# Block-wise linear attention and a gated MLP on one core: two tokens to a row, 64x64 attention tiles, and one written order for every engine

## The chip, the core and the metric

The kernel runs on one core of a Trainium2 chip. The metric is the time of one execution on the device, in microseconds (us), the median of several. The core's engines run side by side and wait for each other by semaphores: TensorE (PE: matmuls, results into PSUM; PEld is its loading of weights), VectorE (DVE), ScalarE (ACT), GpSimd (POOL, which is given no operand in PSUM here), and SyncE (SP), which issues transfers. PSUM has eight banks of 512 fp32 columns on 128 partitions.

## What is computed

Inputs are q, k, v of shape (4 batches, 8 heads, 768 tokens, 64) in fp32, a decay `lam` for each head, and the weights of a gated MLP. The attention has no softmax; a state of 64x64 per head carries the past. In blocks of 64 tokens:

```python
intra = einsum('bhic,bhjc->bhij', qb, kb) * Dmask      # lam ** (i-j) where i >= j, else 0
intra = einsum('bhij,bhjd->bhid', intra, vb)
inter = einsum('bhid,bhde->bhie', qb * lam_pow, kv_state)
out[block] = intra + inter
kv_state = lam ** 64 * kv_state + einsum('bhsd,bhse->bhde', kb * rev_pow, vb)
```

Both kernels take 128 tokens as a block, which gives the same sums. The heads are joined to x of (4, 768, 512), and then:

```python
h = maximum(x @ w_in, 0)                    # 512 -> 1024
u, v = h[..., :512], h[..., 512:]
v_n = (v - mean) / sqrt(var + 1e-6)         # over the 512 features
v_s = einsum('ts,bsd->btd', w_spatial, v_n) + b_spatial[None, :, None]
out = (u * v_s) @ w_out                     # 512 -> 512
```

The mix over tokens (`v_s`) needs all 768 tokens of a batch, so it can start only when the attention of the batch's last tokens is done.

## The kernel before

The work is cut into 12 steps of 256 tokens, three to a batch (`NR`), each of two chunks of 128 tokens (`c`). A step goes through these functions:

- `load_step` (L65): SyncE issues the transfers of q, k and v, fp32, 1.5 MB a step. For k and v a partition holds one token of each chunk, so the runs are 64 floats, 256 bytes (L72, L77). For q a partition holds two neighbouring tokens, 512 bytes (L74). Four steps' inputs fit (`fin`, bufs=4).
- `cast_step` (L144): k times its decay to the block's end becomes `kd` (L150: on VectorE for the first three steps, then on GpSimd); q is cast on ScalarE (L153), v on GpSimd (L154).
- `trans_step` (L157): 16 transposes of 128x128 on PE (L163) into `pt`, a tile of two banks; ScalarE copies the k half (L168), VectorE multiplies the q half by its decay (L170).
- `scores_step` (L177): 16 matmuls with 64 rows, two heads in the two row halves of the array (L189); VectorE applies mask and decay (L192).
- `kv_step` (L198): the chunk's k v sums, 16 matmuls with 64 columns (L207). The state lies in SBUF; VectorE multiplies it by lam^128 (L218) and adds the new sum (L219).
- `out_step` (L222): state times q (L242) on the two diagonal 64x64 tiles, and masked scores times v (L249), added in PSUM; ScalarE writes x transposed (L252).

Then the MLP: `pv` (L269) and `pu` (L292) multiply by the halves of w_in, with the statistics of v on VectorE (L282 to L288). `wt_piece` (L329) transposes w_spatial once. `pvs` (L301) mixes over tokens, for each of 4 groups of 128 features in two halves of 384 tokens: six matmuls and a seventh that adds the bias by a matmul of a constant with the broadcast bias (L309); VectorE multiplies by u (L311). `po` (L316) is the last product; ScalarE evacuates it (L325) and SyncE stores it (L326).

The order on PE and GpSimd is that of the program (`manual_schedule`, L358). In each of its 12 rounds the loop casts step n+2, makes the scores of n+1, the output of n, the state of n+1, and the transposes of n+2; between them `fill` takes MLP pieces from a list, so that the MLP of one batch lies among the attention of the next. The other engines are ordered by the framework's scheduler. The weights are loaded by GpSimd (L108, L360 to L364), cast to bf16 on the way. All PSUM tiles have two banks, four of them in rotation (L54).

Of the kernel before, what the change touches and what calls it, by code (L numbers as in the profile page):

```python
# [13 lines left out]
PE = mybir.EngineType.PE  # L15
# [3 lines left out]
def kernel(  # L19
# [18 lines left out]
    NBLK = S // P  # L38
    NG = H // 2
    NCH = DM // P  # L40
    NR = S // (2 * P)
    NS = B * NR
    T2 = 2 * P
    HW_ = S // 2

    const = ctx.enter_context(tc.tile_pool(name="const", bufs=1))
    wpool = ctx.enter_context(tc.tile_pool(name="wpool", bufs=1))
    fin = ctx.enter_context(tc.tile_pool(name="fin", bufs=4))
    att = ctx.enter_context(tc.tile_pool(name="att", bufs=3))
    gml = ctx.enter_context(tc.tile_pool(name="gml", bufs=1))  # L50
    xpool = ctx.enter_context(tc.tile_pool(name="xpool", bufs=2))
    small = ctx.enter_context(tc.tile_pool(name="small", bufs=2))
    ostg = ctx.enter_context(tc.tile_pool(name="ostg", bufs=3))
    psum = ctx.enter_context(tc.tile_pool(name="psum", bufs=4, space=bass.MemoryType.PSUM))  # L54

    def two_banks(shape, name, dt=FP32):
        return psum.tile(shape, dt, tag="ps", name=name)


    lam_bc = const.tile([P, H], FP32)  # L60
    nc.scalar.dma_start(out=lam_bc, in_=lam.unsqueeze(0).to_broadcast((P, H)))

    st = {}

    def load_step(n):  # L65
        b, r = divmod(n, NR)
        toks = slice(r * T2, (r + 1) * T2)
        q_in = fin.tile([P, H, 2, D], FP32, tag="q_in", name=f"q_in_{n}")
        k_in = fin.tile([P, H, 2, D], FP32, tag="k_in", name=f"k_in_{n}")
        v_in = fin.tile([P, H, 2, D], FP32, tag="v_in", name=f"v_in_{n}")  # L70
        for c in range(2):
            nc.sync.dma_start(out=k_in[:, :, c, :],  # L72
                              in_=k[b, :, toks][:, c * P:(c + 1) * P].rearrange("h p d -> p h d"))
        nc.sync.dma_start(out=q_in.rearrange("p h m d -> p h (m d)"),  # L74
                          in_=q[b, :, toks].rearrange("h (p m) d -> p h (m d)", m=2))
        for c in range(2):
            nc.sync.dma_start(out=v_in[:, :, c, :],  # L77
                              in_=v[b, :, toks][:, c * P:(c + 1) * P].rearrange("h p d -> p h d"))
        st[n] = {"q_in": q_in, "k_in": k_in, "v_in": v_in}

    load_step(0)
    ident = const.tile([P, P], BF16)
    make_identity(nc, ident)

    def iota_f(shape, pattern, base, mult, name):
        ti = const.tile(shape, I32, name=name + "_i")
        nc.gpsimd.iota(ti, pattern=pattern, base=base, channel_multiplier=mult)
        tf = const.tile(shape, FP32, name=name)
        nc.vector.tensor_copy(out=tf, in_=ti)
        return tf  # L90

    krev = iota_f([P, 1], [[0, 1]], P - 1, -1, "krev")

    qpos = iota_f([P, 2, 2, D], [[1, 2], [0, 2], [2, D]], 1, 0, "qpos")

    rel = iota_f([P, 2, D], [[1, 2], [2, D]], 0, -1, "rel")

    win_sb = wpool.tile([P, NCH, DFF], BF16)
    wout_sb = wpool.tile([P, NCH, DM], BF16)
    bsp_bc = wpool.tile([P, S], BF16)  # L100
    wt_sb = wpool.tile([P, NBLK, S], BF16)
    wsp_raw = wpool.tile([P, NBLK, S], BF16)

    def load_win(f0, f1):
        nc.gpsimd.dma_start(out=win_sb[:, :, f0:f1],
                            in_=moe_w_in.rearrange("(g p) f -> p g f", p=P)[:, :, f0:f1])

    load_win(DH, DFF)  # L108
    for n in range(1, 4):
        load_step(n)  # L110


    loglam = const.tile([P, H], FP32)
    nc.scalar.activation(out=loglam, in_=lam_bc, func=AF.Ln)
    logl = const.tile([P, NG], FP32)
    for hh in range(2):
        rows = slice(hh * D, (hh + 1) * D)
        nc.vector.tensor_copy(out=logl[rows, :], in_=loglam[rows, hh::2])
    ldec = const.tile([P, H], FP32)
    nc.scalar.activation(out=ldec, in_=loglam, func=AF.Exp, scale=krev[:, 0:1])  # L120
    lq = const.tile([P, NG, T2], BF16)
    for g in range(NG):
        nc.scalar.activation(out=lq[:, g, :], in_=qpos.rearrange("p m a d -> p (m a d)"),
                             func=AF.Exp, scale=logl[:, g:g + 1])
    l128 = const.tile([P, NG], FP32)
    nc.scalar.activation(out=l128, in_=logl, func=AF.Exp, scale=float(P))
    lm128 = const.tile([P, H], FP32)
    nc.scalar.activation(out=lm128, in_=loglam, func=AF.Exp, scale=-float(P))
    causal = const.tile([P, P], FP32)
    nc.vector.tensor_scalar(out=causal, in0=rel.rearrange("p m d -> p (m d)"), scalar1=0.0,  # L130
                            scalar2=None, op0=ALU.is_ge)
    amask = const.tile([P, 2, 2, 2, P], FP32)
    for h in range(H):
        nc.vector.tensor_scalar(out=amask[:, h // 4, h % 2, (h // 2) % 2, :], in0=causal,
                                scalar1=lm128[:, h:h + 1], scalar2=None, op0=ALU.mult)
    eps_t = const.tile([P, 1], FP32)
    nc.vector.memset(eps_t, 1e-6)
    oo128 = const.tile([P, P], BF16)
    nc.vector.memset(oo128, 1.0 / P)


    xT = {}

    def cast_step(n):  # L144
        s = st[n]
        kd = att.tile([P, 2, H, D], BF16, tag="kd", name=f"kd_{n}")
        qc = att.tile([P, 2, H, D], BF16, tag="qc", name=f"qc_{n}")
        vc = att.tile([P, H, 2, D], BF16, tag="vc", name=f"vc_{n}")
        eng = nc.vector if n < NR else nc.gpsimd
        eng.tensor_tensor(out=kd.rearrange("p c h d -> p h c d"), in0=s["k_in"],  # L150
                          in1=ldec.unsqueeze(2).unsqueeze(3).broadcast_to((P, H, 2, D)),
                          op=ALU.mult)
        nc.scalar.activation(out=qc.rearrange("p m h d -> p h m d"), in_=s["q_in"], func=AF.Copy)  # L153
        nc.gpsimd.tensor_copy(out=vc, in_=s["v_in"])  # L154
        s["kd"], s["qc"], s["vc"] = kd, qc, vc

    def trans_step(n):  # L157
        kd, qc = st[n]["kd"], st[n]["qc"]
        pt = two_banks([P, 2, NG, T2], f"pt_{n}", BF16)
        for j, src in ((0, kd), (1, qc)):  # L160
            for g in range(NG):
                for c in range(2):
                    nc.tensor.transpose(  # L163
                        out=pt[:, j, g, c * P:(c + 1) * P],
                        in_=src[:, c, 2 * g:2 * g + 2, :].rearrange("p h d -> p (h d)"),
                        identity=ident)
# [7 lines left out]
    def qblk(n, g, hh, c):  # L174
        return st[n]["qT"][hh * D:(hh + 1) * D, g, :, c, :]

    def scores_step(n):  # L177


        kT = st[n]["kT"]  # L180
# [237 lines left out]
```

## Time and profile before

| | before |
|---|---|
| time, median of 3 (us) | 184.42 (184.38 to 186.93) |
| span of the profiled execution (us) | 186.7 |
| mean granted clock of TensorE | 0.963 |
| busy us: PE, PEld, DVE, ACT, POOL | 145.7, 96.5, 103.4, 89.1, 34.8 |
| read from and written to memory (MB) | 24.78, 6.29 |
| TensorE matmuls | 1540 |

The page's slices cut the span into 40 equal parts; a digit is the busy share of an engine in a part, in tenths. A line of a timeline has the start in us, the time from first start to last end of the merged instructions, engine, line, operation, output<-inputs, shapes, and in brackets how long the engine stood idle before and what released it. The chain of waits is followed back from the last instruction: at each step to what released it. A matmul's own duration there holds its way through the array; what a matmul costs in a dense row is the distance from start to start.

### The profile page before, as it was taken

The page shows a single profiled execution, that of the slowest core. Times are in us where ns is not written, and L with a number is a line of the kernel's source. Part 1 is how long each engine was busy: PE and PEld are TensorE (multiplying, and loading weights), DVE is VectorE, ACT ScalarE, POOL GpSimd, SP SyncE. Part 2 cuts the span into 40 slices and gives each one's busy share as a digit, 9 for nine tenths or more (in the row PEclk, how much of TensorE's full clock was granted, in tenths as well). Part 3 has the DMA queues.
Part 4 walks back from the last instruction along what each step waited for, and adds up shares of the span by engine and source line. Part 5 has one row for each costly group of instructions (what it writes and reads, how often), then busy time and mean ns, then how long its engine had stood idle before and what let it go on. Part 6 is the DMA issues. An engine that isn't in the chain of part 4 may idle for free.

```text
span 186.7 us, 3638 instructions
## 1 busy us (share of the span) xinstructions
PE 145.7 (78%) x1540; PEld 96.5 (52%) x1540; DVE 103.4 (55%) x191; ACT 89.1 (48%) x98; POOL 34.8 (19%) x35
## 2 busy tenths in 40 slices
PE   0005677507979779999997999999799999999980
PEld 0005563305649556655776665575676646565430
DVE  1029993705399853542989747169884722564400
ACT  4244324712677942268775613666722157660051
POOL 4004060006245344060606005020000000000000
PEclk9999996975999979999999999999999999999999
DMA  4999969999999999999998900530000027000035
GB/s 98 218 211 252 205 161 184 199 212 232 199 241 248 200 239 238 221 225 222 330 254 195 252 8 0 208 133 4 0 0 4 2 79 262 0 0 4 0 132 205
DMA packets 68337, 28.36 MB, mean 152 GB/s; under 512 B 50528, under 2 KB 65248, under 8 KB 68320
## 3 DMA queue, kind: packets, MB, share of 16 engines
q1 hardware_dynamic: 65664, 25.17, 56.5%
q0 software_dynamic: 2512, 2.95, 9.6%
q8 instruction: 12, 0.20, 0.5%
q14 instruction: 5, 0.04, 0.1%
q10 hardware_dynamic: 144, 0.00, 0.0%
HBM read 24.78 MB, written 6.29 MB: 166 GB/s over the span
## 4 chain that ended last, share of the span: by engine, by line
PE 54%; SPq 13%; DVE 11%; ACT 9%; DMA 9%; issue 2%; POOL 1%; ACTq 0%; POOLq 0%
PE pvs L307 17%; PE po L322 11%; DMA v_in<-in_v_dram 9%; PE pv L277 8%; PE pu L297 7%; SPq L77 6%; SPq L72 5%; PE pt L163 4%; DVE a L192 3%; PE pvs L309 3%; SPq L74 3%; DVE st L282 3%; ACT vh L280 2%; ACT wt_sb L336 2%; DVE vn L288 2%
## 5 line engine op out<-in xcount | busy, mean ns | idle before, releaser
L307 PE MATMUL pvs<-wt_sb,vn 128*128 128x384 bf16 x192 | 37.8, 331 | 2.1 <-ACT wt_sb L336 2.0
L192 DVE TENSOR_TENSOR a<-pam,amask 128x1024 bf16<-128x1024 f32 x24 | 28.5, 1210 | 6.0 <-PE pam L189 6.0
L154 POOL CAST vc<-v_in 128x1024 bf16<-128x1024 f32 x12 | 12.9, 1074 | 84.0 <-DMA v_in<-in_v_dram 42.7
L252 ACT ACTIVATE xT<-pat 128x1024 bf16<-128x1024 f32 x12 | 15.8, 1320 | 23.7 <-PE pat L249 23.6
L307 PEld LDWEIGHTS <-vn 128*128 128x128 bf16 x192 | 18.9, 99 | 14.9 <-issue 2.5
L297 PE MATMUL pu<-xT,win_sb 128*128 128x256 bf16 x192 | 24.4, 285 | 1.9 <-DVE a L192 1.9
L311 DVE TENSOR_TENSOR gT<-pvs,uT 128x768 bf16<-128x768 f32 x16 | 15.3, 958 | 18.2 <-PE pvs L309 18.1
L277 PE MATMUL pv<-win_sb,xT 128*128 128x512 bf16 x96 | 24.2, 400 | 1.2 <-ACT xT L252 1.2
L322 PE MATMUL po<-wout_sb,gT 128*128 128x512 bf16 x96 | 21.9, 379 | 1.5 <-DVE a L192 1.1
L297 PEld LDWEIGHTS <-win_sb 128*128 128x128 bf16 x192 | 19.2, 102 | 5.7 <-issue 1.8
L153 ACT ACTIVATE qc<-q_in 128x1024 bf16<-128x1024 f32 x12 | 12.7, 1055 | 19.0 <-DMA q_in<-in_q_dram 19.0
L325 ACT ACTIVATE o<-po 128x1024 f32<-128x1024 f32 x12 | 12.3, 1025 | 19.0 <-PE po L322 19.0
L282 DVE BATCH_NORM_STATS2 st<-vh 128x6 f32<-128x512 bf16 x24 | 15.6, 682 | 10.4 <-ACT vh L280 10.3
L163 PE MATMUL pt<-ident,kd 128*128 128x128 bf16 x96 | 8.6, 242 | 15.5 <-DVE kd L150 15.5
L170 DVE TENSOR_TENSOR qT<-pt,lq 128x1024 bf16<-128x1024 bf16 x12 | 8.2, 684 | 18.5 <-ACT kT L168 18.5
L150 POOL TENSOR_TENSOR kd<-k_in,ldec 128x1024 bf16<-128x1024 f32 x9 | 17.1, 1897 | 6.1 <-DMA k_in<-in_k_dram 6.1
L168 ACT ACTIVATE kT<-pt 128x1024 bf16<-128x1024 bf16 x12 | 12.2, 1021 | 11.2 <-PE pt L163 11.2
L280 ACT ACTIVATE vh<-pv 128x1024 bf16<-128x1024 f32 x12 | 12.3, 1024 | 8.8 <-PE pv L277 8.8
L163 PEld LDWEIGHTS <-kd 128*128 128x128 bf16 x96 | 7.2, 110 | 17.4 <-DVE kd L150 15.7
L277 PEld LDWEIGHTS <-xT 128*128 128x128 bf16 x96 | 9.5, 102 | 11.7 <-issue 1.7
L322 PEld LDWEIGHTS <-gT 128*128 128x128 bf16 x96 | 9.2, 98 | 11.9 <-issue 1.0
L299 ACT ACTIVATE uT<-pu 128x1024 bf16<-128x1024 f32 x12 | 12.2, 1020 | 5.9 <-PE pu L297 5.8
(52 smaller groups left out, 146.2 us busy)
## 6 DMA issues: line engine op xcount, KB each, us to landing
k_in<-in_k_dram SPq DMA_DIRECT2D x24, 256.0 KB, 5.8
q_in<-in_q_dram SPq DMA_DIRECT2D x12, 512.0 KB, 6.1
v_in<-in_v_dram SPq DMA_DIRECT2D x24, 256.0 KB, 6.0
out_dram<-o SPq DMA_DIRECT2D x12, 512.0 KB, 3.4
wsp_raw<-in_moe_w_spatial_dram POOLq DMA_DIRECT2D x1, 1152.0 KB, 11.3
win_sb<-in_moe_w_in_dram POOLq DMA_DIRECT2D x2, 512.0 KB, 8.4
wout_sb<-in_moe_w_out_dram POOLq DMA_DIRECT2D x1, 512.0 KB, 14.8
bsp_bc<-in_moe_b_spatial_dram POOLq DMA_DIRECT2D x1, 192.0 KB, 11.7
```

What stands on the lines that cost most here:

```text
L150: eng.tensor_tensor(out=kd.rearrange("p c h d -> p h c d"), in0=s["k_in"], in1=ldec.unsqueeze(2).unsqueeze(3).broadcast_to((P, H, 2, D)), ...
L154: nc.gpsimd.tensor_copy(out=vc, in_=s["v_in"])
L163: nc.tensor.transpose(out=pt[:, j, g, c * P:(c + 1) * P], in_=src[:, c, 2 * g:2 * g + 2, :].rearrange("p h d -> p (h d)"), identity=ident)
L192: nc.vector.tensor_tensor(out=a_sb[:, i].rearrange("p h g c x -> p (h g) c x"), in0=pam.rearrange("p h g c x -> p (h g) c x"), in1=amask[: ...
L252: nc.scalar.activation(out=xT[b][:, r].rearrange("p g (c d m) -> p (g c) m d", c=2, m=2), in_=po.rearrange("p g c (m d) -> p (g c) m d", m ...
L277: nc.tensor.matmul(out=ps[:, j], lhsT=x[:, r, c, j * P:(j + 1) * P], rhs=win_sb[:, c, DH:DFF], start=(c == 0), stop=(c == NCH - 1))
L280: nc.scalar.activation(out=vh[:, pair, :], in_=ps, func=AF.Relu)
L282: nc.vector.bn_stats(out=m["st6"][:, t, :], in_=vh[:, t, :])
L297: nc.tensor.matmul(out=ps[:, f], lhsT=win_sb[:, c, f * P:(f + 1) * P], rhs=x[:, r, c, :], start=(c == 0), stop=(c == NCH - 1))
L307: nc.tensor.matmul(out=ps[:, i, 0:HW_], lhsT=m["vn"][:, s, f * P:(f + 1) * P], rhs=wt_sb[:, s, cols], start=(s == 0), stop=False)
L311: nc.vector.tensor_tensor(out=m["gT"][:, f, :].rearrange("p (i x) -> p i x", i=2), in0=ps[:, :, 0:HW_], in1=m["uT"][:, f, :].rearrange("p ...
L322: nc.tensor.matmul(out=ps[:, j], lhsT=gT[:, c, t * P:(t + 1) * P], rhs=wout_sb[:, c, :], start=(c == 0), stop=(c == NCH - 1))
```

## The change

The kernel is written anew around four ideas.

*Rows of two tokens.* k, q and v are all loaded with two neighbouring tokens to a partition, in runs of 512 bytes, one load of 512 KB each. A chunk of 128 tokens now lies on 64 partitions, two tokens each; its sums over tokens are done as two matmuls with 64 rows. The columns of w_spatial are transposed with a step of two to fit.

*64x64 attention tiles.* All attention matmuls (`s_c`, `a_v`, `k_v`) use a 64x64 quarter of the array; two heads `o` and two chunks `c` make the four quarters, written to different banks where their rows differ.

*Decays as powers of the position.* v is multiplied at its cast by lam^(384-t) (`v_d`), q at its transpose's evacuation by lam^(t-384) (`e_q`), t counted from the batch's start. Their product has the right power for scores and for the state, so the state needs no decay any more: it is summed in one PSUM bank over the whole batch (`k_v`, bank 7) and only copied out (`s_s`). The mask is 0 and 1.

*One order, written out.* `ORDER` is a list of about 630 operations, each with its step, its bank and its engine; every engine works in this order. PSUM is one tile of eight banks, and each operation names its bank. Evacuations are by single banks and lie on ScalarE or VectorE by the list. `GT` makes GpSimd read an element of a given load before it issues the next weights, so that these come after it.

Besides, the mix over tokens has no bias matmul: VectorE adds the bias in fp32 while it evacuates (`g_b`), and the product with u is an operation of its own, mostly on GpSimd (`g_m`). Inputs are held three deep in place of four.

```diff
+ORDER = """
+LK.0.2.S lam.A pos.P LQ.0.2.S LV.0.2.S LV.1.2.S idn.P LB.6.T msk.P LN.6.A LK.1.2.S KC.0.2.A LL.D LX.A TK.0.6.T
+LQ.1.2.S QC.0.2.P EK.0.6.D LT.0.A TQ.0.6.T LK.2.2.S VD.0.2.P LT.1.A EQ.0.6.D SC.0.1.0.T LT.2.A LQ.2.2.S
...
+SS.0.0.A TQ.1.5.T EK.1.6.A KV.0.1.T LQ.3.2.S GT.0.2.P WI.0.P EQ.1.5.D AV.0.1.0.T SS.0.1.A EX.0.1.1.A
+SC.1.0.2.T KC.2.2.P SC.1.1.4.T EX.0.0.0.A MK.1.0.2.D LV.3.2.S QC.2.2.A GT.1.2.P WI.1.P TK.2.6.T MK.1.1.4.D
...
+"""
...
+    NIN, NCA, NTR, NA, NX, NO, NVS = 3, 2, 2, 2, 3, 4, 2
...
-    psum = ctx.enter_context(tc.tile_pool(name="psum", bufs=4, space=bass.MemoryType.PSUM))
+    ps = psum.tile([P, 8, 512], FP32, name="ps")
+    SB = 7
...
-            nc.sync.dma_start(out=k_in[:, :, c, :],
-                              in_=k[b, :, toks][:, c * P:(c + 1) * P].rearrange("h p d -> p h d"))
+        eng.dma_start(out=dst[n % NIN][:, h0:h1].rearrange("p h m d -> p h (m d)"),
+                      in_=src[b, h0:h1, t].rearrange("h (p m) d -> p h (m d)", m=2))
...
+    def after(e, x, n):
+        nc.gpsimd.tensor_copy(out=seen, in_=(k_in, q_in, v_in)[x][n % NIN][0:1, 0, 0, 0:1])
...
+    def v_d(e, n, x):
+        h = slice(*hx(x))
+        vec(e).tensor_tensor(out=vd[n % NCA][:, h], in0=v_in[n % NIN][:, h],
+                             in1=lv[:, n % NR, h].unsqueeze(3).broadcast_to((P, h.stop - h.start, 2, D)), op=ALU.mult)
...
+    def s_c(e, n, i, b):
+        pa = bank(b, 2).rearrange("p o (w j x) -> p o w j x", w=2, j=2)
...
+                for o in range(2):
+                    for c in range(2):
+                        nc.tensor.matmul(out=pa[row(c), o, w, j], lhsT=kT[n % NTR][row(o), u, j, c * Q64:(c + 1) * Q64],
+                                         rhs=qv(n, o, u, c), start=True, stop=True)
...
+    def k_v(e, n, c):
+        pkv = bank(SB)[:, 0:4 * D].rearrange("p (u d) -> p u d", u=4)
+        new = n % NR == 0 and c == 0
...
+                    nc.tensor.matmul(out=pkv[row(o), u], lhsT=kc[n % NCA][row(c), m, u, o, :],
+                                     rhs=vd[n % NCA][row(c), 4 * o + u, m, :],
+                                     start=new and u == 0 and m == 0, stop=(u == 3 and m == 1),
+                                     skip_group_check=True)
+
+    def s_s(e, n, c):
+        copy(e, s_sb[(2 * n + c) % 4].rearrange("p u d -> p (u d)"), bank(SB)[:, 0:4 * D])
...
-                nc.vector.tensor_tensor(out=sd, in0=prev, in1=lb, op=ALU.mult)
-                nc.vector.tensor_tensor(out=s_sb[:, c], in0=sd, in1=pkv[:, c], op=ALU.add)
...
-            nc.tensor.matmul(out=ps[:, i, 0:HW_], lhsT=oo128, rhs=bsp_bc[:, cols],
-                             start=False, stop=True)
...
+    def g_b(e, bb, f, i, b):
+        HW = S // 2
+        nc.vector.tensor_tensor(out=vsb[(bb * 4 + f) % NVS][:, i * HW:(i + 1) * HW], in0=bank(b)[:, 0:HW],
+                                in1=bsp[:, i * HW:(i + 1) * HW], op=ALU.add)
+
+    def g_m(e, bb, f, i):
...
+        vec(e).tensor_tensor(out=gT[bb % 2][:, f, cols].rearrange("p (a y m) -> p a y m", m=2, y=Q64),
+                             in0=vsb[(bb * 4 + f) % NVS][:, cols].rearrange("p (a y m) -> p a y m", m=2, y=Q64),
+                             in1=uT[bb % 2][:, f, cols].rearrange("p (a m y) -> p a y m", m=2, y=Q64), op=ALU.mult)
...
+    with tc.manual_schedule():
+        for token in ORDER.split():
+            name, *args, e = token.split(".")
+            ops[name](e, *map(int, args))
```

A word of the order is operation, step (or batch), further numbers, bank and engine (A ScalarE, D VectorE, P GpSimd, T TensorE, S SyncE): L loads; KC and QC casts of k and q, VD of v; TK and TQ transposes, EK and EQ their evacuations; SC scores, MK mask; KV states, SS their copy; AV output of the attention, EX its evacuation; PV, PU, PW, PO the products of the MLP, EV, EU, EO their evacuations, BN, RA, RD, VN the normalization, GB bias, GM gate product; WT and EW the transposes of w_spatial; WI, WS, WO, BS the loads of weights and bias; ST stores.

## The prediction

> **What bounds the kernel now.** I read the page's table of engines and its slices first, to see when each engine works.
>
> ```profile
> PE 145.7 (78%) x1540; PEld 96.5 (52%) x1540; DVE 103.4 (55%) x191; ACT 89.1 (48%) x98; POOL 34.8 (19%) x35
> ...
> PE   0005677507979779999997999999799999999980
> ...
> DMA  4999969999999999999998900530000027000035
> ```
>
> TensorE (PE) is nearly full from about the tenth slice (4.67 us each) on and idle or half idle before that, while the DMA engines are full from the second slice to about the 23rd. So there are two stretches with different limits. Next I cut the span into the time before 43.5 us and four pieces after it, of about one batch each (busy time of PE, PEld, DVE, ACT, POOL, then clock, DMA share, GB/s):
>
> ```profile
> 43.50:78.50 35.00, 31.14 (x355) 22.53 (x356) 23.39 (x37) 20.10 (x20) 13.63 (x9) 0.90 1.13 230
> 78.50:113.30 34.80, 33.49 (x385) 22.15 (x380) 23.56 (x44) 20.33 (x22) 8.69 (x6) 1.00 0.85 207
> 113.30:148.00 34.70, 33.40 (x384) 22.25 (x378) 22.54 (x45) 16.63 (x18) 3.93 (x3) 1.00 0.13 47
> 148.00:184.00 36.00, 32.56 (x236) 18.57 (x232) 13.34 (x28) 15.68 (x17) 0.00 (x0) 1.00 0.21 79
> ```
>
> A batch takes 34.8 us and PE is busy 33.4 of it, at full clock: there PE sets the pace, and VectorE with 23 is far behind. Before 43.5 us PE was busy only 145.7 - 130.6 = 15 us, partly at a lower clock. The chain of waits and PE's timeline say why:
>
> ```profile
> 25.91 15.96 DMA v_in<-in_v_dram
> 42.00 1.05 POOL vc L154
> ```
>
> ```profile
> 43.09 0.43 PE L207 MATMUL pkv<-vc,kd 128*64 128x64 bf16 x8 [8.07 <-POOL vc L154]
> ```
>
> The v of step 2 takes 16 us to land, where the median is 6.0. In the records of single packets, 26 to 42 us is the time in which w_spatial, its bias and w_out come in: packets of 256 bytes (18 ns each on one engine) alternate with packets of 1536 or 1024 bytes (134 and 96 ns), so v gets a small part of the engines.
>
> **What the Trainium skill says.** "TensorEngine Tiling (Array Packing)", section Key Properties: tiles of the array load weights and multiply in parallel, and changing the tiling mode drains the engine. The trace agrees on both for two tiles. PE's timeline around one step:
>
> ```profile
> 122.47 0.62 PE L189 MATMUL pam<-qT,kT 64*128 64x128 bf16 x16
> 123.02 0.63 PE L242 MATMUL pat<-qT,s 64*64 64x128 bf16 x16
> 123.59 0.64 PE L249 MATMUL pat<-a,vc 128*64 128x128 bf16 x16
> 124.06 0.42 PE L207 MATMUL pkv<-vc,kd 128*64 128x64 bf16 x16
> 124.41 1.92 PE L297 MATMUL pu<-xT,win_sb 128*128 128x256 bf16 x16
> ```
>
> From start to start the groups of 16 take 0.55, 0.57, 0.47 and 0.35 us. In the trace's single starts two matmuls begin 3.5 ns apart and the next two 56 ns later (32 ns for pkv, 64 columns), whether they are two row halves (L189) or two column halves (L249); where the mode changes, 147 ns pass in place of 56, so a change costs about 0.1 us. Four tiles at once appear nowhere in this trace.
>
> "SBUF — State Buffer", section Who interferes with whom: a VectorE instruction in a two-port mode, or with two SBUF inputs, locks out GpSimd and the reverse; one with at most one SBUF input does not. The trace agrees; GpSimd's timeline, then VectorE's:
>
> ```profile
> 43.81 1.90 POOL L150 TENSOR_TENSOR kd<-k_in,ldec 128x1024 bf16<-128x1024 f32 x1 [0.77 <-DMA k_in<-in_k_dram]
> ...
> 51.16 1.90 POOL L150 TENSOR_TENSOR kd<-k_in,ldec 128x1024 bf16<-128x1024 f32 x1 [0.71 <-DMA k_in<-in_k_dram]
> ```
>
> ```profile
> 44.09 2.09 DVE L288 TENSOR_SCALAR vn<-vh,mv,rstd 128x512 bf16<-128x512 bf16 x2
> ...
> 51.36 1.27 DVE L282 BATCH_NORM_STATS2 st<-vh 128x6 f32<-128x512 bf16 x2
> ```
>
> vn beside kd takes 2.09 us for two in place of 0.73; the statistics beside kd take their usual time.
>
> **The change part by part: PE.** From the same timeline, start to start: pv and po 0.2166 us a matmul, pu 0.1156, pvs 0.1625, transposes 0.0557. Unchanged: 192 x 0.2166 + 192 x 0.1156 + 192 x 0.0557 = 41.6 + 22.2 + 10.7 = 74.5 us. Mixing: 224 matmuls become 192 because the bias moves to VectorE, 36.4 to 31.2 us. Scores: 96 pairs of 64x128 tiles become 96 quads of 64x64 tiles, 5.4 us before and, if four tiles run in the time of two, 5.4 after. Attention times v: the same, 5.4 and 5.4. State times q: 160 matmuls used two diagonal tiles (80 pairs, 4.5 us) and can now use all four (40 quads, 2.2). States: each chunk of 128 tokens is summed as two of 64 rows, so 160 matmuls (80 pairs of 32 ns, 2.5 us) become 320 (5.1). Transposed w_spatial: 2.0 both times. Mode changes: 4 a step, 48, before; 55 in the written order after; 4.8 and 5.5. Sum before 135.5 us, after 131.3. The upper bound for a quad is two pairs after each other, 112 ns: 232 quads x 0.056 = 13 us more. I take 56 ns, because row halves and column halves are each shown to run together.
>
> **The other engines.** Counting the instructions of the order by engine. VectorE: 24 masks x 1.21 (L192), 12 q products x 0.68 (L170), 24 statistics x 0.77 (L282, L283), 24 vn x 0.53 (L288), 32 bias additions of 384 columns (half of L311's 768 in 0.96: 0.56), 12 reciprocals, and 27 evacuations of a bank (0.39 for 256 columns at L215; 0.55 to 0.68 estimated for the wider ones) with four gate products of 0.5: 29.0 + 8.2 + 18.5 + 12.7 + 17.9 + 1.9 + 18.2 = 106 us. What goes is the decay of the state (L218 and L219, 15.8 us) and the gate product at L311. ScalarE: evacuations of 512 columns at about 0.6 (estimated from 1.02 for 1024 and 1.46 for 1536, L168 and L336), in all 80 us. GpSimd: 12 v products x 1.9 (L150), 15 casts x 1.08 (L154), 28 gate products of 384 columns at 0.71 (1.9 x 384/1024), since they read uT with a stride perhaps up to 1.4: 59 to 79 us. None comes near PE's 131. GpSimd at 45% busy holds up only vn and four gate products on VectorE: some 0.2 us each, 6 us. The smaller evacuations lie beside PE as the larger ones do now. The decay tables and masks are made at the start, under the first loads.
>
> **Transfers.** k and v move in runs of 512 bytes in place of 256: 27 ns a packet in place of two of 18. 12 x 3 loads x 1024 packets x 27/16 ns = 62 us of all engines where it was 76. Weights are held back: GpSimd reads one element of a chosen load before it issues them. That is an added wait. Queued behind the first (k of step 2) stand the k cast of step 2, which needs the same load, then v's product of step 2, and PE's transposes wait for the former: it costs nothing while the load it names lands before what is queued behind it could start. The other added hop is in the gate: matmuls, bias on VectorE, product on GpSimd, then po; 0.56 + 0.71 + hops, some 1.4 us against 0.96 now. Behind pvs stand four more halves of the same batch (0.98 each), so it is hidden but for the last one, some 0.5 us.
>
> **The start.** First packet at 2.4 us (now too). A load of 512 KB takes 1.7 us, and k of step 2 is seventh: 14 us. Its cast (1.1), eight transposes (0.45 to 0.9), q's, the product (0.7) and the scores put PE at about 19; half of w_in, released by that load, needs 0.95 for issue and 3.1 alone (512 packets x 96/16), some 4 beside q and v: also 19 to 20. So the first pv runs at 20 us; it is at 29.76 now. From there I let PE run on, with 3.5 us lost: some 2.5 at q of step 3, which shares the engines with weights until about 30 us, and 1 at the lower clock. The whole of w_spatial should be there at 36 us, when PE has just used up the work that does without it.
>
> **The sum.** By 20 us PE has done the attention of steps 0 and 1 and part of 2: 2 x 2.8 + 1.3 = 6.9 us of its 131.3. Left 124.4. 20 + 124.4 + 3.5 + 4.5 (waits in the rest: 4%, as in the windows above) + 4.3 (tail: now 5.2 from the last po to the end, less 0.4 for a half as wide evacuation and 0.5 for a half as large store) = 156.7 us of span. The profiled run is 186.7 where the median is 184.4, so 155 us of time.
>
> **The rivals.**
> *Evacuations hold PE back (167).* VectorE has 25 us of work per batch of some 33, in finer pieces and an order fixed for every engine, so a late one holds what is queued behind it. For it: three waits a batch on the mask product even now (0.93 the longest, before pu at 135.07). Against: ScalarE and GpSimd have room. With 5 us a batch in place of 1.2: +12, 167.
> *Quads run as pairs (168).* +13 us, above. For it: no quad in the trace. Against: the separate pairs.
> *Slower: VectorE and GpSimd shut each other out throughout, or readers of PSUM, now one tile of eight banks, wait for all that was written before.* The first: 106 + 79 + 14 us until data flow = 199. The second: evacuations and PE take turns, 131 + some 138 of evacuation + hops, 270 or more. For the second: the q product waits for the k copy now (18.5 us in all), though they lie in different banks of one tile. Against the first: the lines at 51 us.
>
> **How the numbers follow.** The sum above 0.63, evacuations 0.17, quads as pairs 0.11, slower 0.09. The range from 148 (no waits in the start or later, a weight half 2 us sooner) to 172 (either middle rival with a longer start) leaves out the slow rival and both middle ones together. Faster 0.90, within 2% 0.02, slower 0.08.
>
> **What would show it.** First pv near 20 us; PE's windows of a batch about 33 us; four score matmuls starting within some 15 ns and the next 56 ns later; no load over about 8 us beside the held weights; vn a little over 0.5 us. Wrong would be: waits of PE on the mask, bias or gate products of over 2 us a batch, quads 112 ns apart, or PE idle between 24 and 40 us for want of w_spatial.

## The result and the profile after

The changed kernel takes 161.34 us (median of 4, 159.30 to 162.21) where the kernel before, run beside it, took 185.12: a ratio of 0.866, 95% interval 0.857 to 0.875. Forecast were 155.0 and a range of 148 to 172. Its executions come in two groups, 159.3 us at a mean granted clock of 0.989 and 161 to 162 at 0.979, so ratios compare only the quicker executions of each kernel, and a difference of under 2 us between two versions of it isn't read from a few runs.

The page of the kernel after, engines and slices (4.0 us each):

```profile
PE 138.3 (86%) x2073; PEld 91.0 (57%) x2090; DVE 108.2 (68%) x191; ACT 82.4 (52%) x154; POOL 77.7 (49%) x91
...
PE   1256764999899998999999999999999999999990
...
PEclk9999995699999999999999999999999999999999
...
DMA  3999999999999998266999951530000000134055
```

TensorE is full from the eighth slice on and stays so to the end; before, the fullness began later and was broken in the middle. Slices 6 and 7 are 6 and 4 tenths busy, and the clock of slices 7 and 8 reads 5 and 6. VectorE at 108 us, ScalarE at 82 and GpSimd at 78 are all far from PE. The same cut as before, the start and then about a batch each (busy time of PE, PEld, DVE, ACT, POOL, then clock, DMA share, GB/s):

```profile
0.00:25.90 25.90, 11.57 (x299) 9.76 (x300) 12.03 (x19) 15.95 (x31) 15.07 (x26) 0.97 1.05 248
25.90:62.00 36.10, 34.49 (x513) 23.00 (x519) 28.73 (x50) 21.60 (x38) 16.17 (x18) 0.93 1.11 266
62.00:94.00 32.00, 30.59 (x458) 20.02 (x454) 24.66 (x43) 16.68 (x32) 20.17 (x24) 1.00 0.81 229
94.00:126.00 32.00, 31.68 (x618) 21.47 (x624) 26.19 (x45) 16.08 (x32) 13.76 (x15) 1.00 0.18 65
126.00:155.70 29.70, 29.48 (x205) 16.73 (x208) 16.54 (x35) 11.21 (x21) 12.56 (x12) 1.00 0.21 80
```

After 94 us PE misses 0.5 us in 61.7. The two spans differ by 186.7 - 159.9 = 26.8 us, in three parts: PE runs on from 25.9 us where before it did from 43.5 (17.6); from there to the last `po` it is 130.2 us where it was 138.0 (7.8); the end after that is 3.8 us where it was 5.2 (1.4). Two thirds of the difference thus lie before PE runs on, but not all of that is idle time saved, since PE had been busy 15.1 us by 43.5 in the kernel before and 11.6 by 25.9 in this one. Counted by PE's idle time, the start gives 14.1 us (28.4 to 14.3), about half; 7.4 us are less busy time of PE (145.7 to 138.3), and the rest is fewer waits later and the shorter end.

What ends the start now, from the chain of waits (start, length, what), and PE's timeline there:

```profile
8.84 7.37 DMA k_in<-in_k_dram
16.38 9.47 DMA win_sb<-in_moe_w_in_dram
```

```profile
25.90 0.58 PE L385 MATMUL ps<-win_sb,xT 128*128 128x512 bf16 x1 [3.29 <-DMA win_sb<-in_moe_w_in_dram]
26.70 5.38 PE L385 MATMUL ps<-win_sb,xT 128*128 128x512 bf16 x14 [0.22 <-issue]
```

The v of step 2 is no longer what PE waits for; it is the first half of w_in, for 3.3 us, and behind the wait 16 matmuls of 512 columns take 6.1 us in place of 3.5 (0.2166 each).

The attention's small tiles in the middle of a dense stretch:

```profile
104.84 0.31 PE L350 MATMUL ps<-qT,s_sb 64*64 64x128 bf16 x8
104.98 0.39 PE L359 MATMUL ps<-a_sb,vd 64*64 64x128 bf16 x16
105.20 0.62 PE L313 MATMUL ps<-qT,kT 64*64 64x128 bf16 x32
105.65 0.41 PE L329 MATMUL ps<-vd,kc 64*64 64x64 bf16 x16
```

From start to start, 8 matmuls take 0.14 us, 16 take 0.22, 32 take 0.45. In the single starts four matmuls begin within 10 ns (105.204, .208, .211, .214) and the next four 56 ns later (105.260): four quarters run in the time of two halves.

Three groups off PE (busy us, mean ns of one | idle before it, and what ended it):

```profile
L456 POOL TENSOR_TENSOR gT<-vsb,uT 128x384 bf16<-128x384 f32 x28 | 30.1, 1096 | 28.5 <-DVE vsb L450 23.6
...
L450 DVE TENSOR_TENSOR vsb<-ps,bsp 128x384 f32<-128x384 f32 x32 | 17.3, 549 | 5.6 <-PE ps L445 5.1
...
L414 DVE TENSOR_SCALAR vn<-vh,mv,rstd 128x512 bf16<-128x512 bf16 x24 | 16.5, 723 | 0.3
```

The bias addition costs VectorE 0.55 us, the gate product costs GpSimd 1.10, and vn takes 0.72, since ten of the 24 take 0.68 us or more and the others 0.4.

### The profile page after: what moved, and what is told of

Same layout as the page of the kernel before. It is cut to its first block, busy times and chain, and to the rows that moved or that the text cites. A ratio compares the mean times of both kernels' runs of the same rounds, so it can differ in the third digit from the quotient of the medians.

```text
span 159.9 us, 4876 instructions
## 1 busy us (share of the span) xinstructions
PE 138.3 (86%) x2073; PEld 91.0 (57%) x2090; DVE 108.2 (68%) x191; ACT 82.4 (52%) x154; POOL 77.7 (49%) x91
## 4 chain that ended last, share of the span: by engine, by line
PE 54%; DMA 15%; DVE 12%; SPq 5%; POOL 5%; issue 4%; ACT 3%; DVEq 0%; ACTq 0%; POOLq 0%
PE ps L462 13%; PE ps L423 11%; PE ps L385 10%; PE ps L445 8%; DMA win_sb<-in_moe_w_in_dram 6%; SPq L184 5%; DMA q_in<-in_q_dram 5%; DMA k_in<-in_k_dram 5%; POOL gT L456 4%; DVE vsb L450 4%; PE ps L284 3%; DVE vn L414 3%; PE ps L313 2%; PE ps L329 2%; PE ps L359 2%
## 5 line engine op out<-in xcount | busy, mean ns | idle before, releaser
L456 POOL TENSOR_TENSOR gT<-vsb,uT 128x384 bf16<-128x384 f32 x28 | 30.1, 1096 | 28.5 <-DVE vsb L450 23.6
L445 PE MATMUL ps<-wt_sb,vn 128*128 128x384 bf16 x192 | 33.7, 326 | 0.2 <-DVE vsb L450 0.2
L317 DVE TENSOR_TENSOR a_sb<-ps,m 128x1024 bf16<-128x1024 f32 x24 | 28.7, 1218 | 6.0 <-PE ps L313 5.0
L276 POOL TENSOR_TENSOR vd<-v_in,lv 128x1024 bf16<-128x1024 f32 x12 | 22.8, 1904 | 16.0 <-DMA q_in<-in_q_dram 6.4
L385 PE MATMUL ps<-win_sb,xT 128*128 128x512 bf16 x85 | 24.9, 412 | 4.1 <-DMA win_sb<-in_moe_w_in_dram 3.3
L423 PE MATMUL ps<-xT,win_sb 128*128 128x256 bf16 x192 | 24.2, 273 | 0.3 <-DVE wt_sb L170 0.3
L462 PE MATMUL ps<-wout_sb,gT 128*128 128x512 bf16 x90 | 21.6, 379 | 0.3
L450 DVE TENSOR_TENSOR vsb<-ps,bsp 128x384 f32<-128x384 f32 x32 | 17.3, 549 | 5.6 <-PE ps L445 5.1
L390 ACT ACTIVATE uT<-ps 128x512 bf16<-128x512 f32 x22 | 12.9, 600 | 10.1 <-PE ps L423 10.1
L414 DVE TENSOR_SCALAR vn<-vh,mv,rstd 128x512 bf16<-128x512 bf16 x24 | 16.5, 723 | 0.3
```

The costliest lines, as they stand in the source:

```text
L276: vec(e).tensor_tensor(out=vd[n % NCA][:, h], in0=v_in[n % NIN][:, h], in1=lv[:, n % NR, h].unsqueeze(3).broadcast_to((P, h.stop - h.start ...
L317: nc.vector.tensor_tensor(out=a_sb[n % NA][:, i].rearrange("p o w j x -> p (o w) (j x)"), in0=bank(b, 2).rearrange("p o (w y) -> p (o w) y ...
L385: nc.tensor.matmul(out=bank(b), lhsT=x[:, c, g], rhs=win_sb[:, g, DH:DFF], start=(g == 0), stop=(g == NCH - 1))
L390: nc.scalar.activation(out=o, in_=i, func=AF.Relu)
L414: vec(e).tensor_scalar(out=vn[p2][:, t], in0=vh[p2][:, t], scalar1=mv[p2][:, t, 0:1], scalar2=rstd[p2][:, t:t + 1], op0=ALU.subtract, op1= ...
L423: nc.tensor.matmul(out=pu[:, f2].rearrange("p (c x) -> p c x", c=2), lhsT=win_sb[:, g, f * P:(f + 1) * P], rhs=x[:, :, g, :], start=(g == ...
```

## The experiments

The working theory after the result: the gain is the sum of a shorter start (shorter transfers, held weights) and less PE work (bias, quads). The rival: the written order of the evacuating engines is what carries it, and the parts don't add. (To evacuate is to copy a result from its PSUM bank to SBUF, after which PE may write that bank again; ScalarE and VectorE do it.) All ratios are to the kernel before, run on the same chip. Results per run are medians.

**Quads undone?** The attention loops run over the column halves of one row half first, so that program order holds pairs.

```diff
-            for j in range(2):
-                for o in range(2):
+            for o in range(2):     # in s_c; in a_v the loops become o, i, w and c, i, j, w
+                for j in range(2):
```

> The changed kernel with the same attention matmuls in another order: two column halves of one row half follow each other, so that the next two matmuls use the same two quarters again and only two run at once. Theory (a quad of 64x64 tiles costs what a pair costs, 56 ns, and PE sets the pace): 232 groups of four become 464 of two, 232 x 0.056 = 13 us more, some 174 us. Rival (four tiles gain nothing over two, or PE does not set the pace): no change, within 2 us of 161.

160.87 us, 0.864 (0.855 to 0.873): the same. The timeline says why:

```profile
99.76 0.31 PE L350 MATMUL ps<-qT,s_sb 64*64 64x128 bf16 x8
99.90 0.42 PE L359 MATMUL ps<-a_sb,vd 64*64 64x128 bf16 x16
100.16 0.41 PE L329 MATMUL ps<-vd,kc 64*64 64x64 bf16 x16
```

8 still take 0.14 us and 16 about 0.26: PE starts matmuls of the other row half ahead of their turn. The edit took nothing away, so it doesn't price the quads; the starts above do.

**Bias back on PE**, as a seventh matmul of a constant with the bias in bf16; `g_b` then only copies.

```diff
...
+        nc.tensor.matmul(out=bank(b)[:, 0:HW], lhsT=oo128, rhs=bsp[:, i * HW:(i + 1) * HW],
+                         start=False, stop=True)
...
-        nc.vector.tensor_tensor(out=vsb[...], in0=bank(b)[:, 0:HW], in1=bsp[...], op=ALU.add)
+        nc.vector.tensor_copy(out=vsb[...], in_=bank(b)[:, 0:HW])
```

> The changed kernel with the bias back on PE: a seventh matmul of 384 columns in each of the 32 groups of the mix over tokens, and VectorE only copies. Theory (PE sets the pace from the first pv on): 32 x 0.1625 = 5.2 us more, 166.5 us. Rival (VectorE or GpSimd sets the pace in the mix stage): no change, since VectorE's instruction stays as long as it was.

164.82 us, 0.886 (0.879 to 0.894): 3.5 us slower than the change between the medians, where 32 matmuls of 0.1625 us cost 5.2. The bias's load leaves SyncE's queue by this edit, and the transposes of w_spatial start 1.2 us earlier (42.79 in place of 44.04), which may give part back; no run shows that apart. The term of the sum is shown in kind, its size only roughly.

**Runs of 256 bytes.** Each load as two transfers, one for each token of the row.

```diff
-        eng.dma_start(out=dst[n % NIN][:, h0:h1].rearrange("p h m d -> p h (m d)"),
-                      in_=src[b, h0:h1, t].rearrange("h (p m) d -> p h (m d)", m=2))
+        for m in range(2):
+            eng.dma_start(out=dst[n % NIN][:, h0:h1, m],
+                          in_=src[b, h0:h1, t].rearrange("h (p m) d -> p h m d", m=2)[:, :, m])
```

> The changed kernel with each load of 512 KB issued as two of 256 KB, one per token of a row, so that the runs are 256 bytes. Theory (the start is bound by transfers, 18 against 27 to 32 ns a packet, so a load takes 2.3 in place of 1.8 us): k of step 2, the seventh load, lands some 3.5 us later, the weights that wait for it too, and the first pv runs at about 30 in place of 26 us; 4 to 8 us more, 165 to 169. Rival (the start is bound by the chain of casts, transposes and evacuations): first pv within 1 us of 26 and no change.

178.27 us, 0.957 (0.946 to 0.967): 17 us slower, over twice the most expected. The start is only 1.7 us later; the loss is in the middle:

```profile
65.31 1.03 PE L285 MATMUL ps<-ident,qc 128*128 128x128 bf16 x8 [3.58 <-ACT qc L168]
...
83.17 0.42 PE L360 MATMUL ps<-a_sb,vd 64*64 64x128 bf16 x16 [1.17 <-POOL vd L277]
...
86.67 3.60 PE L386 MATMUL ps<-win_sb,xT 128*128 128x512 bf16 x8 [3.08 <-ACT xT L168]
```

With slower transfers the loads stay behind for over 100 us, and the fixed order waits for each late cast. The mean granted clock falls too, from 0.979 to 0.941: of the 17 us some 7 are time lost to the clock (estimated, 0.059 x 176.6 less 0.021 x 159.9, as if PE were busy in all of it). In the changed kernel the transfers seem just fast enough; its order has little room.

**All weights at the start**, without the held issues.

```diff
-LK.0.2.S lam.A ... idn.P LB.6.T msk.P LN.6.A ... GT.0.2.P WI.0.P ... GT.1.2.P WI.1.P ...
+LK.0.2.S lam.A ... idn.P LB.6.T msk.P WI.0.P WI.1.P WS.1.P WS.0.P WO.P LN.6.A ...
```

> The changed kernel with all weights issued at the start on GpSimd, in the same order, and no holding back. Theory (holding the weights back is what keeps k, q and v at their full rate): v of step 0 and what follows land late, as v of step 2 did in the kernel before; the attention of steps 0 to 2 moves by 8 us or more, first pv at 30 us or later, 5 to 12 us more in all. Rival (the sum of bytes decides, not their order): w_in is there early and w_spatial too, the total stays within 2 us, or falls by up to 4 since the weights no longer come last.

169.29 us, 0.912 (0.904 to 0.920): 8 us slower, as expected. PE's timeline has the waits, both for casts of step 1, which stood waiting for their loads (the cast of k for 6.9 us). GpSimd's five issues in a row take 3.9 us themselves, but its first cast comes only 0.7 us later for it, so it is the transfers that hold PE up:

```profile
23.57 1.03 PE L275 MATMUL ps<-ident,kc 128*128 128x128 bf16 x8 [8.39 <-POOL kc L163]
...
29.12 1.03 PE L275 MATMUL ps<-ident,qc 128*128 128x128 bf16 x8 [4.52 <-ACT qc L159]
```

**w_in earlier**, without `GT`: its first half right behind the masks, the second behind the k cast of step 1, and the first `pv` ahead of the transposes of step 2.

```diff
-... GT.0.2.P WI.0.P ... GT.1.2.P WI.1.P TK.2.6.T ... VD.2.2.P PV.0.1.6.T EX.1.0.0.D PV.0.0.1.T
+... msk.P WI.0.P ... KC.1.2.P WI.1.P ... PV.0.1.6.T PV.0.0.1.T TK.2.6.T ...
```

> The changed kernel with the two halves of w_in issued right at the start and after the k cast of step 1, not held back, and the pv of step 0 moved ahead of the transposes of step 2 on PE. Theory (the 26 us to the first pv are the landing of k of step 2 at 16.2, 3.8 us from issue to the first packet of w_in, and 5.7 us of packets mixed with the loads): the first pv runs at 17 to 20 us, the other loads come 3 to 6 us later, and some 2 to 4 us are gained, 157 to 159 us. Rival (only the sum of bytes until the PE is fed counts): the later loads take back what is gained, within 1.5 us of 161.

161.61 us, 0.867 (0.861 to 0.873): no gain. The first `pv` does run at 20.69 us, but:

```profile
25.33 0.31 PE L350 MATMUL ps<-a_sb,vd 64*64 64x128 bf16 x8 [0.72 <-DVE a_sb L308]
...
29.40 0.59 PE L376 MATMUL ps<-win_sb,xT 128*128 128x512 bf16 x1 [2.24 <-DVE xT L161]
```

PE now waits for step 1 behind it. That fits a start that is bound by the sum of what has to arrive until about 30 us, not by the place of one load.

**The order of ScalarE, VectorE and SyncE given back to the framework's scheduler**; the order on PE and GpSimd, the tiles and the loads stay.

```diff
-    with tc.manual_schedule():
+    with tc.manual_schedule(engines={mybir.EngineType.PE, mybir.EngineType.Pool}):
```

> The changed kernel with the written order kept on PE and GpSimd alone, as in the kernel before; ScalarE, VectorE and the issuing of transfers are ordered by the framework's scheduler. Theory (the gain comes from the start, the bias and the transfers, and evacuations have room): within 3 us of 161. Rival (the written order of the evacuating engines is what took PE's waits from some 9 us after the start to 3): 8 us more or worse.

186.26 us over 20 executions, and a ratio of 0.988 (0.984 to 0.992), which stands for some 184 us: nearly the whole gain is gone. The profile is of an execution of 188.06 us, so its waits are read and not its sums. In windows of the trace the start is no worse (PE busy 13.4 us by 26.0), but from 26 to 62 PE is busy 19.8 us, where the change has 34.5 in the same stretch. One wait is 11 us of it:

```profile
48.73 0.63 ACT L168 ACTIVATE qc<-q_in 128x512 bf16<-128x512 f32 x1 [11.12 <-DMA q_in<-in_q_dram]
49.27 0.58 ACT L390 ACTIVATE uT<-ps 128x512 bf16<-128x512 f32 x1
...
49.90 0.64 PE L313 MATMUL ps<-qT,kT 64*64 64x128 bf16 x16 [11.26 <-ACT uT L390]
```

Read from the top: a cast of q stands at the head of ScalarE's queue until its load lands; the evacuation of u behind it had its data at 38.3, and PE needs the bank that it would free. Later waits of PE are 2.1, 2.0 and 2.7 us; before the last two, what stands ahead on ScalarE is an evacuation of `po` that waits 2.2 and 2.5 us for an earlier store to free its tile. The mean granted clock of this execution is 0.933. The expectation took the placing of evacuations as worth 3 us at most; this is the largest miss of the study, and it names what the sum had no term for.

**The gate product without its stride** (u and vsb taken in the order in which they lie, so the product pairs wrong tokens; the work is the same).

```diff
-        vec(e).tensor_tensor(out=gT[...].rearrange("p (a y m) -> p a y m", m=2, y=Q64), ...
-                             in1=uT[...].rearrange("p (a m y) -> p a y m", m=2, y=Q64), op=ALU.mult)
+        vec(e).tensor_tensor(out=gT[...], in0=vsb[...], in1=uT[...], op=ALU.mult)
```

> The changed kernel with the gate product reading u and writing without the step of 64 between neighbouring tokens; the tokens of u and v are then not those of each other, so the output is not the reference's. Theory: GpSimd's product falls from 1.10 to about 0.71 us (1.9 x 384/1024), 11 us of its 78, but PE sets the pace, so within 1 us of 161. Rival (GpSimd's chain to po is on the path): 3 us or more gained.

159.70 us (158.29 to 161.25). The product falls from 1096 to 917 ns, not to 710. The 1.6 us lie within the spread of the change's own runs; the last experiment decides it.

Now the same parts from the other side, added one by one to the kernel before.

**Before, with w_spatial, its bias and w_out issued behind the casts of step 2.**

```diff
-        nc.gpsimd.dma_start(out=wsp_raw, ...)     # and bsp_bc, wout_sb: ahead of the loop
             if n + 2 < NS:
                 cast_step(n + 2)
+            if n == 0:
+                nc.gpsimd.dma_start(out=wsp_raw, ...)     # and bsp_bc, wout_sb
```

> The kernel before with one part of the change alone: w_spatial, its bias and w_out are issued on GpSimd after the casts of step 2, so after v of step 2 has landed. Theory (the 8.07 us wait of PE on v of step 2 is the small share that v has beside these weights): the wait is gone, v of step 2 lands at about 30, w_spatial still comes before its transposes at 59, 8 us less, 177 us. Rival (the wait moves to the loads of steps 3 and 4 or to w_spatial): within 2 us of 185.

188.41 us, 1.012 (1.003 to 1.020): no gain. ScalarE's timeline, then PE's:

```profile
50.64 1.06 ACT L153 ACTIVATE qc<-q_in 128x1024 bf16<-128x1024 f32 x1 [8.74 <-DMA q_in<-in_q_dram]
51.60 1.28 ACT L252 ACTIVATE xT<-pat 128x1024 bf16<-128x1024 f32 x1
```

```profile
52.94 0.61 PE L277 MATMUL pv<-win_sb,xT 128*128 128x512 bf16 x1 [9.52 <-ACT xT L252]
```

The wait of 8 us at 43 us is gone and one of 9.5 us has come: another cast that waits for its load, ahead of an evacuation.

**Before, with k and v in runs of 512 bytes.**

```diff
-        for c in range(2):
-            nc.sync.dma_start(out=k_in[:, :, c, :],
-                              in_=k[b, :, toks][:, c * P:(c + 1) * P].rearrange("h p d -> p h d"))
+        nc.sync.dma_start(out=k_in.rearrange("p h m d -> p h (m d)"),      # v the same
+                          in_=k[b, :, toks].rearrange("h (p m) d -> p h (m d)", m=2))
```

> The kernel before with one edit: k and v are loaded in rows of two tokens (512-byte runs, as q already is) and nothing else is moved, so that the tokens in a tile are not those that the masks stand for and the output is not the reference's; the work of every engine is unchanged. Theory that the transfer rate is the larger part of the gain (a k or v load in 1.8 us of the queue's time instead of 2.3, four megabytes of k and v in all): 170 to 177 us, with the first pv matmul of the main stretch 3 to 6 us earlier. Rival, that the order of the evacuating engines has to change with it, because a cast that waits for its load stands ahead of an evacuation in ScalarE's queue: 181 to 186 us.

193.82 us, 1.050 (1.042 to 1.058): slower, which neither theory allowed for. The page's slices (4.8 us) show that the transfers did become quicker, full to the 17th slice (81 us) where they were to the 23rd (107 us):

```profile
PE   0030636029747977999997999999989999999990
...
DMA  3999999999999999908400000260000008000035
```

ScalarE's timeline, then PE's, show where it went:

```profile
39.12 1.06 ACT L151 ACTIVATE qc<-q_in 128x1024 bf16<-128x1024 f32 x1 [13.02 <-DMA q_in<-in_q_dram]
40.08 1.28 ACT L250 ACTIVATE xT<-pat 128x1024 bf16<-128x1024 f32 x1
```

```profile
41.42 0.61 PE L275 MATMUL pv<-win_sb,xT 128*128 128x512 bf16 x1 [9.70 <-ACT xT L250]
```

This is the fourth cast of q, that of step 3, and the first xT, that of step 0. In the kernel before the scheduler put that xT ahead of the third cast; after the edit of the loads it put it behind the fourth. Besides, w_spatial is issued at 19.1 in place of 25.4, because the v cast ahead of it on GpSimd ran sooner, and now shares the engines with the q that ScalarE waits for. The rival's mechanism holds, and its size was too small.

**Before, weights late, and ScalarE in written order**, each cast of q just ahead of its step's transposes.

```diff
-        nc.scalar.activation(out=qc..., in_=s["q_in"], func=AF.Copy)      # in cast_step, for n >= 2
+                q_cast(n + 2, st[n + 2]["qc"])
                 trans_step(n + 2)
...
-    with tc.manual_schedule(engines={PE, mybir.EngineType.Pool}):
+    with tc.manual_schedule(engines={PE, mybir.EngineType.Pool, mybir.EngineType.Activation}):
```

> The kernel before with its weights for the gate held back as in before_late_w, and with ScalarE in a written order in which the cast of q of step n+2 stands just ahead of that step's transposes, behind the evacuations of step n. Theory that the wait of 9.5 us in before_late_w was a cast at the head of ScalarE's queue: that wait falls below 2 us and the time is 176 to 180 us. Rival, that PE only waits for the same load one operation later (the transposes need the cast): 185 to 189 us.

206.75 us, 1.122 (1.115 to 1.129). The wait of 9.5 us is gone; no wait of PE after 31 us is over 4 us. But ScalarE now waits elsewhere, and PE for ScalarE (engine, line, what for: us in all, times, longest), first this kernel, then the kernel before:

```profile
ACT rstd L288 <- DVE mv L287: 23.5, 12, 3.3
PE pt L167 <- ACT qc L145: 16.4, 7, 3.9
```

```profile
ACT rstd L284 <- DVE mv L283: 3.1, 6, 1.0
PE pt L163 <- ACT qc L153: 1.1, 1, 1.1
```

The program's text has the square root of a `pv` right behind its evacuation, where it waits for VectorE's statistics, and all that ScalarE owes PE stands behind it, twelve times. One case: the root waits 1.57 us until 100.50, the cast of q runs behind it at 100.70, and PE's transposes start at 101.80 after 3.88 us. So PE does wait for the cast one operation later, as the rival said, though mostly not for the load but for what stands ahead of the cast. By these traces it isn't a written order as such that gains, but one in which nothing that waits stands ahead of something that PE needs. Neither theory had named the root.

Last, two experiments on what the start of the changed kernel still loses.

**PE kept busy over the wait for w_in**, by 14 matmuls on constants into the bank that the next matmul overwrites.

```diff
+        if n == 0 and c == 1:
+            for _ in range(14):
+                nc.tensor.matmul(out=bank(b), lhsT=ident, rhs=lq[:, 0, 0:2]..., start=True, stop=True)
```

> The changed kernel with 14 matmuls of 128x512 on constants put ahead of the second pv row of the start, where PE waits 3.3 us for the input weight; they write a bank that the following matmul overwrites. Theory that the idle stretch costs twice, once as a wait and once because the 16 matmuls after it run at a low granted clock (about 6.1 us instead of 3.5): 158.5 to 159.5 us, the pv matmuls after the wait at about 0.22 us each. Rival, that the loads behind it bound PE at the start anyway, or that the clock falls for another reason than idleness: 161 to 162 us.

158.10 us (157.62 to 158.56), 0.856 (0.854 to 0.859). PE's timeline:

```profile
22.64 2.97 PE L386 MATMUL ps<-lq,ident 128*128 128x512 bf16 x13 [0.16 <-issue]
25.70 3.61 PE L389 MATMUL ps<-win_sb,xT 128*128 128x512 bf16 x16
```

One of the 14 has no record. The first `pv` starts at 25.70 (25.90 without them), and the 16 take 3.6 us in place of 6.1. All slices of the granted clock read 9, and no execution is above 158.6. The gain is 2.5 us in the records and 3.2 between the medians. In the change's profile the clock reads half from 24.3 to 31.1 us and full elsewhere, which makes its mean of 0.979; the executions at 0.989 fit half as long a stretch. This agrees with the Trainium skill, "TensorE: Matmul & The Clock Gate", section Why this matters for your kernels, which advises against gaps of over some 3 us between matmuls: the gap here was 3.3. The edge isn't measured here: in the run with w_in earlier the clock is half from 29.1 to 32.5 us behind a wait of 2.24. And PEclk reads 9 in places where PE isn't at full pace: eight transposes take 1.04 us at 14.55 in the changed kernel and 0.62 at 18.54, all under a 9. With all weights at the start, eight still take 1.03 us at 29.12 and 0.62 at 32.42, so the waits of 8.4 and 4.5 us before that, which leave every slice at 9, met a PE that wasn't at full pace yet. The change's transposes before its gap ran at the quicker pace.

**The same, with u stored in token order**, by two evacuations in place of one, so that the gate product has no stride and still pairs the right tokens.

```diff
-        relu(e, uT[...][:, 2 * j:2 * j + 2, ...], bank(b).rearrange("p (f x) -> p f x", f=2))
+        for f in range(2):
+            relu(e, uT[...][:, 2 * j + f, ...].rearrange("p (a y m) -> p a m y", m=2, y=Q64),
+                 bank(b).rearrange("p (f a m y) -> p f a m y", f=2, a=2, m=2)[:, f])
...
```

> As warm, and with u written in token order at its evacuation (two evacuations of one bank each in place of one of two), so that the gate product of GpSimd reads and writes without a stride of 64. Theory that the product of 1.10 us comes to 0.7 to 0.8 and GpSimd's shorter holds give VectorE and PE 1.6 us, as the contiguous product alone gave: 1 to 2 us below warm, 157 to 158.5 us. Rival, that the stride only moves to the evacuation, which holds PE's banks longer, and that two instructions cost 0.2 us more than one on an engine with a third of its time free: 0 to 1 us above warm.

157.96 us (157.36 to 158.50), 0.856 (0.852 to 0.859): the same as without it. The page's group:

```profile
L461 POOL TENSOR_TENSOR gT<-vsb,uT 128x384 bf16<-128x384 f32 x28 | 25.3, 917 | 27.9 <-DVE vsb L455 24.6
```

GpSimd does 4.7 us less, ScalarE 3.0 more, and the time stays: neither amount is on the path that sets the end. The 1.6 us of the product without its stride were thus no gain that shows at full clock.

## Why the prediction was right, and where it was not

*What bounds the kernel: right.* PE sets the pace in both kernels after the start; no other engine's sum matters.

*The sum.* It gave a span of 156.7 us and the profiled one is 159.9. Its terms, predicted and measured: first `pv` 20 and 25.9 (+5.9); from there to the last `po` 124.4 + 3.5 + 4.5 = 132.4 and 130.2 (-2.2); tail 4.3 and 3.8 (-0.5). These make the 3.2. The terms partly offset each other: PE had been busy 11.6 us by its later start, where the sum has 6.9 done by 20, and it waited less than the 4% put down for it. Another 3.1 came from turning span into time: the prediction set the profiled span of before (186.7) against a median that belongs to shorter executions (184.42) and took 1.7 off, where each execution's time is about 1.7 above its own span (161.64 for 159.9).

*The start: mechanism right, size wrong.* "k of step 2 is seventh: 14 us" was 16.2: with the queue full a packet of 512 bytes takes 32 ns, not 27. "0.95 for issue and 3.1 alone, some 4 beside q and v" was 9.5 us from issue to landing: 3.7 until the first packet moved, and then 5.8 in which packets of 1024 bytes (96 ns) and of 512 (now 40 ns) come about one for one, 139 to 138 from 22 to 23 us. The Trainium skill, "DMA: Bandwidth & Descriptors", section SWDGE vs HWDGE vs iDMA, says that an engine takes turns between its queues; the trace agrees. Its figure for the first byte of a GpSimd transfer, about 1 us (section Specifications), isn't what this trace shows. The prediction had read that alternation at w_spatial and didn't price it at w_in. Sharing isn't all of it: each of the five weight transfers ends with 16 packets of 4 bytes, one for each engine as it seems, and for this one 15 of them lie between 23.0 and 24.2 us and the last at 25.5. By these records one late engine holds PE for some 1.3 of its 3.3 us (an estimate); why it is late stays open. The lower clock, "1" of the 3.5 us, cost 2.5.

*Waits of 4%: too many.* The last 61.7 us lose 1%.

*PE's work.* Quads at 56 ns: right, by the starts. Bias off PE: 5.2 predicted, 3.5 between the medians when it is taken back, which moved a load as well. The rest (state times q, states, mode changes) wasn't tried apart.

*The other engines: near enough.* VectorE 106 and 108, ScalarE 80 and 82, GpSimd 59 to 79 and 78. vn was 0.53 and is 0.72, the gate product 0.71 to 1.4 and is 1.10; without its stride still 0.92, so most of the miss isn't the stride. The product isn't on the path, as the last experiment shows; vn wasn't tried apart.

*Transfers.* "No load over about 8 us" was wrong for half of the v loads (median 8.6); w_spatial landed at 42.4, not 36, and cost PE little, since the late start had left it work.

*The rivals.* Evacuations that hold PE back, quads as pairs, and engines that shut each other out did not come. But the first saw half of the matter: it named the fixed order as the risk, and with slower loads it is one (178 us). The runs show the order also as what the gain rests on: the same tiles, loads and operations in the scheduler's order take 184 to 186 us. Nothing in the sum would have told that kernel from this one, so that the time came near the forecast is in part luck.

*What the prediction had no term for: the parts don't add.* Taken from the changed kernel, the order costs some 23 us by the ratio, the longer runs 17, the held weights 8, the bias 3.5: 51 us for a gain of 24. Given one at a time to the kernel before, held weights and longer runs cost 2 and 9 us by the ratios. The traces point to the reason: PE is fed through ScalarE's and GpSimd's queues, in which casts that wait for loads and evacuations that PE waits for stand in one line. A shorter transfer helps only where no cast of a later step stands ahead, and a good line only where the loads arrive about when it expects them. Quicker loads with a worse line gave 193.8 us, a good line with slower loads 178.3. Which of the moves in the order carries how much stays open, and so does the order of VectorE and SyncE apart from ScalarE's.

## What to carry to other kernels

When PE waits for an evacuation, look at what stood ahead of it in the evacuating engine's queue: a cast that waits for a load costs PE that load's lateness, even though PE needs nothing of it, and speeding up some loads can make it worse. Credit a rewrite's parts together, since each may be worth nothing alone and most of the gain when taken away. A wait of PE can cost a second time through its clock: here one of 3.3 us cost 2.5 more, and matmuls on constants took that part back.

## What the runs showed that was not expected

- PE doesn't keep to program order between tiles of different row halves. In the changed kernel the states (L329) stand ahead of the operation with L350 in the order, and yet, in PE's timeline:

```profile
21.85 0.32 PE L329 MATMUL ps<-vd,kc 64*64 64x64 bf16 x10
21.99 0.24 PE L350 MATMUL ps<-qT,s_sb 64*64 64x128 bf16 x2
22.01 0.23 PE L329 MATMUL ps<-vd,kc 64*64 64x64 bf16 x4
```

  All 16 of this operation of L329 use row half 1 of the array; six of them start after the first of L350, whose first two use row half 0. In the reordered attention PE itself put the row halves side by side. The Trainium skill, "TensorE: Matmul & The Clock Gate", section The mechanism, has matmuls start in strict order; these starts disagree with it.
- A transfer that GpSimd issued while the SyncE queue was full moved its first packet 3.7 us after the issue began; in the kernel before it was 2.0 to 2.6 us.
- A packet's time on an engine depends on what else is queued: 512 bytes took 27, 32 or 40 ns, 256 bytes 18 or 31.
